# Pads that place the tiles of DMA transfers at multiples of 64 bytes, in an attention and mixture-of-experts kernel

## The chip, the cores and the metric

One core of a Trainium2 chip runs the whole program. The metric is the device time of one execution in microseconds; the time before is the median of three runs.

## The reference

Linear attention is followed by a mixture of experts. For 8 batches and 8 heads of 576 rows with 64 elements:

```
phi(x): p = x @ w_phi;  p = p - max|p|;  [exp(p), exp(-p)]          # 64 -> 256 features
kv = phi(k)^T v;  z = sum of phi(k) over the rows
attn = (phi(q) kv) / (phi(q) z + 1e-6)
x = attn, with the heads side by side                                # 4608 x 512
logits = x @ w_gate                                                  # 8 experts
each (token, expert) in falling order of logits; a token goes to its first expert with room (576)
out[tokens of e] = relu(x[tokens of e] @ w1[e]) @ w2[e]
```

All inputs and the output are fp32.

## The kernel before

**Attention.** The work is cut into 16 units of two batches and two heads. For each unit, `loadx` (L130) fetches k and q into `ki` and `qi` with four DMAs each (`raw`, L116 to 122). One such DMA fills 32 partitions with 36 runs of 32 fp32 values, 128 bytes a run. `loadv` (L123 to 129) fetches v into `vi` in runs of 256 bytes. DVE transposes 32x32 blocks into `kT` and `qT` (L174); PE projects them (L185, tile `g` in PSUM); DVE takes the maximum of the absolute values (L189, tiles `kgm` and `qgm`) and subtracts it (L192, or ACT and POOL at L198 and L201); ACT takes the exponentials into `kP` (L213) and `qP` (L280); PE forms kv (L231), spreads it (L247) and multiplies it with `qP` (L293, the num block, 144 matmuls a unit, `qP` stationary and `kz` moving). DVE divides into a tile `xp` (L309) of 9 rows of 576 bytes a partition, whose bytes 32 to 543 of each row are stored to `xs` in DRAM in runs of 512 bytes (`st`, L312 to 315); the other bytes are parts of the logits.

`ki`, `qi`, `vi`, `kT`, `qT`, `kz` and `xp` have two buffers each, so that the loads of a unit wait for the buffers of the unit two before. The order of all of this is a table of due times, from which the planner `Plan` writes one order for each engine and for SP's queue.

**Routing and experts.** The routing counts logits by digits to find the order of the tokens (`routing`, L582 on). For each of 8 experts, weights are loaded in four chunks for w1 (`raww10` to `raww13`, runs of 1024 bytes) and four for w2 (`raww20` to `raww23`, runs of 2048 bytes) at L767, split into a high and a low part by ACT (L838) and DVE (L841, L842; tiles `w1h`, `w1l`, `w2h`, `w2l`, four each), while POOL gathers the tokens' rows from `xs` into `xg` (L853). From the third expert on, `xg` goes through DRAM (`xd`) and comes back transposed into the tile `xl`. PE computes `h` from `xh`, `xl` (L923) and `y` from `fh`, `fl` (L954), with 576 tokens an expert; the last 64 tokens go through `ff` (L969). ACT copies `y` to `ysb` (L977), and POOL scatters it to the output (L984). The experts follow one another.

**Where tiles lie.** A tile pool reserves a place for each name when it is first asked for, one behind the other, in each partition's memory, and starts every tile at a multiple of 32 bytes. The pools of the first stages (`const`, `mc`, `rt`, `xp` and others) lie first; the attention's pool `att` and the FFN's pool `ffn` use the same memory after them, one after the other in time. The starts, modulo 64, that the program has before and after the change:

| tile | what uses it | before | after |
|---|---|---|---|
| `ki`, `qi` (both buffers) | loads of k and q | 32 | 0 |
| `vi` (both) | loads of v | 0 | 0 |
| `xp`, bytes that a store reads | stores, units 0 to 14 | 0 | 0 |
| `xp` of the last unit, the same | its stores | 32 | 0 |
| `raww10`, `raww11` | loads of w1, chunks 0 and 1 | 0 | 0 |
| `raww12`, `raww13`, `raww20` to `raww23` | the other weight loads | 32 | 0 |
| `xg`, `xl` | gathers, transposed loads | 32 | 0 |
| `ysb` (both) | scatters of the output | 32 | 0 |
| `w`, `bd` | three small loads at the start | 32 | 32 |
| `kT`; `qT` | DVE and PE | 32; 0 | 0; 0 |
| `kz` (two buffers, in turn) | PE, moving | 32, 0 | 0, 32 |
| `xh`, `fh`, `fl`, `ff`, `w1h` to `w2l` | PE, ACT, DVE | 32 | 0 |

`ki` and `qi` start at 224 modulo 256 before and at 0 after; the weight, `xg`, `xl` and `ysb` tiles start at 0 or 32 modulo 256 before, and at 0 after.

Of the kernel before, what the change touches and what calls it, by code (L numbers as in the profile page):

```python
# [7 lines left out]
F32 = mybir.dt.float32  # L8
F32R = mybir.dt.float32r
BF = mybir.dt.bfloat16  # L10
# [87 lines left out]
def attention(ctx, tc, nc, q, k, v, w_phi, w_gate, xs, L, C, xp, cfg={}, after=None, later=None, count=None, init=iter(())):  # L98
# [5 lines left out]
    sb=ctx.enter_context(tc.tile_pool(name='att',bufs=2))  # L104
    ps=ctx.enter_context(tc.tile_pool(name='aps',bufs=1,space=PS))
    ident=C['ident']
    V,A,G,PE=nc.vector,nc.scalar,nc.gpsimd,nc.tensor
# [32 lines left out]
    def pair(u_):  # L140
        return lambda x: ps.tile([128,2,512],F32,name='g%d'%x['buf'][u_],bufs=1)
# [11 lines left out]
    def unit(u):  # L153
        bp,hp=divmod(u,NP)
        t0=u*d['TI']
        def add(name,eng,dur,due,fn,deps=(),mode=None,slot=(),frees=(),lat=None,after=0.,seq=None,ins=0.):
            due=place(name,eng,u,t0+due)
            P.add((name,u),eng,dur,due,fn,[(x,u) for x in deps],
                  lat={'PE':220.,'DVE':95.,'ACT':100.,'POOL':30.,'SP':0.,'X':0.}[eng] if lat is None else lat,mode=mode,slot=slot,frees=frees,after=after,seq=seq and (seq,u),ins=ins)
# [16 lines left out]
        def project(nm,g,s0,s1,due,src):  # L176
            n=s1-s0
            def pe(x):
                p=T[nm+'p',u,g]=pair(('g',u,nm,g))(x)
                t=T[src,u].rearrange('p b s t l -> p b s (t l)')  # L180
                for s in range(s0,s1):
                    for a in range(2):
                        r=slice(64*a,64*a+64)
                        for bi in range(2):
                            PE.matmul(p[64*bi:64*bi+64,a,128*(s-s0):128*(s-s0)+128],t[r,bi,s,:],C['w'][r,:],start=True,stop=True)  # L185
            vw=lambda: T[nm+'p',u,g][:,:,0:128*n].rearrange('p a (s f) -> p a s f',f=128)
            def mx(x):
                m=T[nm+'m',u,g]=sb.tile([128,2,n,1],F32,name=nm+'m',bufs=3)
                V.tensor_reduce(m,vw(),axis=AX.X,op=OP.max,apply_absolute_value=True)  # L189
            def sub(x):  # L190
                t=T[nm+'t',u,g]=sb.tile([128,2,n,128],F32,name=nm+'t',bufs=NT[nm])
                V.tensor_sub(t,vw(),T[nm+'m',u,g].to_broadcast([128,2,n,128]))  # L192
            add((nm,g),'PE',n*(218. if not first else d['cold'][nm]),due,pe,[(src[0]+'t',0),(src[0]+'t',1)],'Q',slots(('g',NG,nm,g)),((src,u),),ins=16*n+.5)
            add((nm+'m',g),'DVE',dv(256*n),due+.8,mx,[(nm,g)])
            if (nm,g) in POOLS and not first:
                def cp(x):
                    t=T[nm+'t',u,g]=sb.tile([128,2,n,128],F32,name=nm+'t',bufs=NT[nm])
                    A.copy(t.rearrange('p a s f -> p a (s f)'),T[nm+'p',u,g][:,:,0:128*n])  # L198
                def gs(x):
                    t=T[nm+'t',u,g]  # L200
                    G.tensor_sub(t,t,T[nm+'m',u,g].to_broadcast([128,2,n,128]))  # L201
                add((nm+'c',g),'ACT',40+ac(256*n),due+1.6,cp,[(nm+'m',g)],slot=slots((nm+'t',NT[nm],g)),frees=(('g',u,nm,g),))
                add((nm+'s',g),'POOL',1450.,due+2.4,gs,[(nm+'c',g)])
            else: add((nm+'s',g),'DVE',dv(256*n),due+1.6,sub,[(nm+'m',g)],slot=slots((nm+'t',NT[nm],g)),frees=(('g',u,nm,g),))
# [79 lines left out]
        for g,(j0,j1) in enumerate(JG):  # L284
            n=j1-j0; due=d['num']+d['ns']*g
            js=sorted(set(j//3 for j in range(j0,j1)))
            def pe(x,g=g,j0=j0,j1=j1):
                p=T['np',u,g]=pair(('g',u,'num',g))(x)
                for a in range(2):
                    for j in range(j0,j1):  # L290
                        for fh in range(2):
                            for ab in range(2):
                                PE.matmul(p[64*ab:64*ab+64,a,73*(j-j0):73*(j-j0)+73],T['qP',u,j//3][:,fh,a,ab,j%3,:],T['kz',u][:,a,fh,ab,:],start=fh==0,stop=fh==1)  # L293
            def dve(x,g=g,j0=j0,j1=j1,n=n):
                p=T['np',u,g][:,:,0:73*n].rearrange('p a (j e) -> p a j e',e=73)
                rd=sb.tile([128,2,n,1],F32,name='rd',bufs=2)
                V.tensor_scalar(rd,p[:,:,:,72:73],1e-6,None,op0=OP.add)
                V.reciprocal(rd,rd)
                if g==0: T['x',u]=(xp if lastu else sb).tile([128,9,144],F32,name='xp',bufs=1 if lastu else 2)
                x_=T['x',u]  # L300
                Lb=L[:,9*bp+j0:9*bp+j1,:]
                if lastu:
                    L3=C['L3'][:,j0:j1]
                    for a in range(2): V.tensor_mul(L3[:,:,:,1+a],p[:,a,:,64*a:64*a+8],rd[:,a].to_broadcast([128,n,8]))
                    V.tensor_reduce(Lb.rearrange('p j (e o) -> p j e o',o=1),L3,axis=AX.X,op=OP.add)
                    if g==1: after()
                    for a in range(2):
                        for j in range(n): A.activation(x_[:,j0+j,8+64*a:72+64*a],p[:,a,j,8-8*a:72-8*a],AF.Copy,scale=rd[:,a,j,:])
                else: V.tensor_mul(x_[:,j0:j1].rearrange('p j (a e) -> p a j e',a=2),p[:,:,:,0:72],rd.to_broadcast([128,2,n,72]))  # L309
            add(('num',g),'PE',n*515.,due,pe,['zk']+[('ex',j) for j in js],'B',slots(('g',NG,'num',g)),tuple(('qP',u,j) for j in js)+(('kz',u),),ins=32*n)  # L310
            add(('x',g),'DVE',(430+dv(144*n)) if not lastu else 900.,due+2.7,dve,[('num',g)],seq=('x',0) if g else None,slot=slots(('xb',2)) if g==0 else (),frees=(('g',u,'num',g),))
# [247 lines left out]
def moe(ctx, tc, nc, L, xs, w1, w2, out, C, MC, R0, rt, cfg={}):  # L559
# [3 lines left out]
    V,G,A,PE=nc.vector,nc.gpsimd,nc.scalar,nc.tensor  # L563
    rp=rt
    fp=ctx.enter_context(tc.tile_pool(name='ffn',bufs=2))
# [16 lines left out]
    def routing(r):  # L582

        last = r==E-1
        wide = r<cfg.get('wide',1)
        if not last:
# [4 lines left out]
            for i,(sh,bits) in enumerate(DIG):  # L591
# [5 lines left out]
                else:  # L597
                    cmp=S([128,NT//n,K,n],f'cmp{K}',BF,b=2)
                    cv=c.rearrange('p (g i) -> p g i',i=n)
                    g=0  # L600
                    for ck in ((WC if K==32 else WC2) if wide else (9,)*(1 if K==32 else 2)):
                        V.tensor_tensor(cmp[:,g:g+ck],cv[:,g:g+ck,None,:].to_broadcast([128,ck,K,n]),
                                        kt[i].rearrange('p (k i) -> p k i',i=n)[:,None].to_broadcast([128,ck,K,n]),op=OP.is_ge); g+=ck
                if wide and i==3: V.memset(fp.tile([1,1],BF,name='wv',bufs=1),0.0)
                if 'rest' in R:
                    with tc.issue_after(R['last']):
                        if i: 
# [90 lines left out]
        lo=S([128,18,64,2],'cmp64',BF,b=2)  # L698
        l2=sf[:,0].rearrange('p (g i) -> p g i',i=2)
        g0=0  # L700
        for lk in (7,7,4) if wide else (9,9):
            g=g0; g0+=lk
            V.tensor_tensor(lo[:,g:g+lk],l2[:,g:g+lk,None,:].to_broadcast([128,lk,64,2]),
                            kl.rearrange('p (k i) -> p k i',i=2)[:,None].to_broadcast([128,lk,64,2]),op=OP.is_equal)
        if wide:

            wk=fp.tile([1,1],BF,name='wk',bufs=1); G.tensor_copy(wk,lo[0:1,0,0,0:1])
        yield
        p=rps([128,9,2,2])
        for g in range(18):  # L710
# [87 lines left out]
    for r in range(1,E):  # L798
# [4 lines left out]
        for i,x in enumerate(z):  # L803
            def f(y,it=it): next(it,None)
            nm=('idx',r) if i==ni else ('up',r) if i>ni else ('rt',r,i)
            if len(x)>2 and x[2]=='ei':

                nm=('ei',r)
# [188 lines left out]
def tile_kernel(ctx, tc, q, k, v, w_phi, moe_w_gate, moe_w1, moe_w2, out):  # L997
# [7 lines left out]
    C['L3'] = L3  # L1005
    C['xd'] = dp.tile([576, 512], F32, name='xd')
    xp = ctx.enter_context(tc.tile_pool(name='xp', bufs=2))
    rp = ctx.enter_context(tc.tile_pool(name='mc', bufs=1))
    rt = ctx.enter_context(tc.tile_pool(name='rt', bufs=1))
    MC, R0 = [], {}  # L1010
# [45 lines left out]
```

## Time and profile before

| | |
|---|---|
| median of 3 runs | 770.24 us (769.56 to 770.79) |
| the profiled execution's own time | 773.05 us |
| its span, first to last instruction | 771.0 us |
| PE, DVE, ACT, POOL busy | 738.6, 572.3, 348.2, 312.0 us |
| mean granted TensorE clock | 0.973 of full speed |
| DMA | 236,944 packets, 94.28 MB; 185,904 packets under 512 bytes |

Attention fills about the first 283 us of the span, the routing the time up to about 310, the experts the rest. PE's busy time is high throughout, and DMA's share is high in the attention stage alone, so a row has to be read with the stretch that it comes from. DMA packets of several queues that wait for one another on an engine are counted each, so that a share can be over 1. A mean time of a packet is worked out from a queue's row as share x length of the stretch x 16 engines / packets; completion marks of a few bytes count as packets too.

### The profile page before, as it was taken

How to read it: one execution, taken by the hardware profiler on the slowest of the kernel's cores; microseconds unless marked ns; L12 is line 12 of the kernel's file. 1: busy time of each engine (PE TensorE's matmuls, PEld its weight loads, DVE VectorE, ACT ScalarE, POOL GpSimd, SP SyncE). 2: the span in 40 equal slices, each digit the busy share in tenths (PEclk: the TensorE clock that was granted, in tenths of full speed). 3: DMA queues.
4: the chain of work that ended last, by engine and by line, in shares of the span. 5: the costliest groups of instructions: out<-in, count | busy, mean ns of one | idle time of the engine just before them, and what ended most of it. 6: DMA issues, size and time to landing. Idle time of an engine off the chain costs nothing.

```text
span 771.0 us, 25322 instructions
## 1 busy us (share of the span) xinstructions
PE 738.6 (96%) x10832; PEld 638.0 (83%) x10832; DVE 572.3 (74%) x1496; ACT 348.2 (45%) x612; POOL 312.0 (40%) x336
## 2 busy tenths in 40 slices
PE   7799999999999976899999999999999999999997
PEld 4578898899988864698898898898898897898995
DVE  5798889998997986788598598597597696673410
ACT  2476766787677640433333333333333423442411
POOL 6587888998889820201302302302202203311002
PEclk9899999999999995899999999999999999999999
DMA  9999889989985131334604504504505505762401
GB/s 135 139 138 147 140 143 173 168 140 149 162 147 116 25 93 56 119 110 140 203 1 147 196 2 150 193 1 155 187 2 167 176 2 170 242 193 71 131 14 48
DMA packets 236944, 94.28 MB, mean 122 GB/s; under 512 B 185904, under 2 KB 223184, under 8 KB 236832
## 3 DMA queue, kind: packets, MB, share of 16 engines
q1 hardware_dynamic: 225552, 71.91, 43.6%
q0 software_dynamic: 6608, 20.16, 8.5%
q8 instruction: 85, 1.39, 0.8%
q10 hardware_dynamic: 4672, 0.59, 0.8%
q14 instruction: 27, 0.22, 0.1%
HBM read 72.58 MB, written 20.05 MB: 120 GB/s over the span
## 4 chain that ended last, share of the span: by engine, by line
PE 70%; issue 12%; DVE 8%; SPq 3%; DMA 2%; POOL 2%; ACT 1%; POOLq 0%; DVEq 0%
PE h L923 21%; PE y L954 18%; PE g L293 9%; PE g L185 5%; PE g L231 4%; PE y L969 3%; DVE kgm L189 3%; SPq L122 3%; PE g L276 2%; PE rps L619 1%; PE g L247 1%; DVE qgm L189 1%; DVE qgt L192 1%; PE rps L615 1%; PE g L260 1%
## 5 line engine op out<-in xcount | busy, mean ns | idle before, releaser
L984 POOL DMA_INDIRECT out_dram<-ysb,idx x40 | 39.3, 981 | 337.2 <-ACT ysb L977 331.2
L222 POOL TENSOR_TENSOR ks<-ks,kP 128x512 f32<-128x512 f32 x112 | 143.2, 1279 | 7.4 <-ACT kP L213 0.2
L923 PE MATMUL h<-xh,w1l 128*128 128x272 f32 (+3 forms) x512 | 142.5, 298 | 0.0
L923 PE MATMUL h<-xh,w1h 128*128 128x272 f32 (+3 forms) x512 | 142.5, 303 | 0.0
L936 ACT ACTIVATE fh<-h 128x272 fp32r<-128x272 f32 (+2 forms) x128 | 48.9, 384 | 137.3 <-PE h L923 129.5
L954 PE MATMUL y<-w2h,fh 128*128 128x512 f32 x256 | 101.1, 398 | 0.0
L954 PE MATMUL y<-w2l,fh 128*128 128x512 f32 x256 | 99.8, 394 | 0.0
L954 PE MATMUL y<-w2h,fl 128*128 128x512 f32 x256 | 99.2, 392 | 0.0
L923 PEld LDWEIGHTS h<-xh,w1h 128*128 128x128 f32 x512 | 96.5, 190 | 2.9 <-ACT fh L936 1.1
L923 PEld LDWEIGHTS h<-xh,w1l 128*128 128x128 f32 x512 | 97.6, 191 | 1.0
L923 PE MATMUL h<-xl,w1h 128*128 128x272 f32 (+3 forms) x512 | 93.4, 299 | 0.0
L213 ACT ACTIVATE kP<-kgt 128x768 f32<-128x768 f32 x96 | 73.9, 837 | 33.4 <-POOL kgt L201 18.9
L940 DVE SCALAR_TENSOR_TENSOR fl<-h,fh 128x272 fp32r<-128x272 f32 (+2 forms) x128 | 53.0, 416 | 39.5 <-ACT fh L936 23.1
L293 PE MATMUL g<-kz,qP 128*64 128x73 f32 x2304 | 79.2, 229 | 2.4 <-DVE kz L262 1.6
L280 ACT ACTIVATE qP<-g 128x768 f32<-128x768 f32 x96 | 71.1, 813 | 21.1 <-PE g L276 21.1
L293 PEld LDWEIGHTS g<-kz,qP 128*64 128x64 f32 x2304 | 76.4, 138 | 4.4 <-DVE kz L262 1.7
L923 PEld LDWEIGHTS h<-xl,w1h 128*128 128x128 f32 x512 | 76.8, 190 | 0.6
L231 PE MATMUL g<-kP,vi 64*64 64x256 f32 x1152 | 71.3, 377 | 0.3 <-PE g L185 0.2
L977 ACT COPY ysb<-y 128x512 f32<-128x512 f32 (+1 forms) x40 | 21.8, 546 | 99.6 <-issue 55.3
L954 PEld LDWEIGHTS y<-w2l,fh 128*128 128x128 f32 x256 | 48.2, 188 | 9.0
L954 PEld LDWEIGHTS y<-w2h,fl 128*128 128x128 f32 x256 | 48.1, 188 | 8.8
L954 PEld LDWEIGHTS y<-w2h,fh 128*128 128x128 f32 x256 | 48.3, 189 | 8.2
(221 smaller groups left out, 1323.7 us busy)
## 6 DMA issues: line engine op xcount, KB each, us to landing
raww<-in_moe_w_dram SPq DMA_DIRECT2D x64, 512.0 KB, 5.2
xs<-xp SPq DMA_DIRECT2D x32, 288.0 KB, 4.7
ki<-in_k_dram SPq DMA_DIRECT2D x62, 144.0 KB, 4.8
qi<-in_q_dram SPq DMA_DIRECT2D x62, 144.0 KB, 4.7
vi<-in_v_dram SPq DMA_DIRECT2D x56, 144.0 KB, 4.7
vi<-in_v_dram POOLq DMA_DIRECT2D x8, 144.0 KB, 7.9
xl<-xd SPq DMA_DIRECT2D x4, 288.0 KB, 4.6
xd<-xg SPq DMA_DIRECT2D x4, 256.0 KB, 2.9
```

The source lines that it names most:

```text
L185: PE.matmul(p[64*bi:64*bi+64,a,128*(s-s0):128*(s-s0)+128],t[r,bi,s,:],C['w'][r,:],start=True,stop=True)
L189: V.tensor_reduce(m,vw(),axis=AX.X,op=OP.max,apply_absolute_value=True)
L213: for i in range(2): A.activation(o[:,:,:,128*i:128*i+128],t,AF.Exp,scale=1.0-2*i)
L222: else: G.tensor_add(ks,ks,kP[:,s])
L231: PE.matmul(p[64*a:64*a+64,i,0:256],v_[r,a,s,:],kP[r,s,a,:],start=s==0,stop=s==8,skip_group_check=True)
L280: for fh in range(2): A.activation(t[:,fh].rearrange('p i a s t -> p i (a s t)'),p,AF.Exp,scale=1.0-2*fh)
L293: PE.matmul(p[64*ab:64*ab+64,a,73*(j-j0):73*(j-j0)+73],T['qP',u,j//3][:,fh,a,ab,j%3,:],T['kz',u][:,a,fh,ab,:],start=fh==0,stop=fh==1)
L923: PE.matmul(p,ws[:,k,o:o+128],xx[:,k,o1:o2],start=n==0,stop=n==11)
L936: A.activation(hh[:,f,o1:o1+m1],p[:,0:m1],AF.Relu)
L940: V.scalar_tensor_tensor(hl[:,f,o1:o1+m1],p[:,0:m1],0.0,hh[:,f,o1:o1+m1],op0=OP.max,op1=OP.subtract)
L954: PE.matmul(p,hx[:,f,o:o+128],ws[:,f%2,:],start=n==0,stop=n==23)
L984: st=G.indirect_dma_start(out=ov,out_offset=bass.IndirectOffsetOnAxis(ap=iv,axis=0),in_=yv,in_offset=None)
```

## The change

Reservations are added or enlarged, and nothing else is touched. In the attention's pool three tiles are asked for that no instruction uses: one behind `kgm`, one behind `qgm` (160 bytes a partition each) and one behind `rd` (32 bytes); in the pool `xp` one of 32 bytes. The tiles `wv` and `wk` in the FFN's pool become 128 elements (256 bytes) in place of one, of which only the first is used, as before.

```diff
             def mx(x):
                 m=T[nm+'m',u,g]=sb.tile([128,2,n,1],F32,name=nm+'m',bufs=3)
+                if u==0 and g==0: sb.tile([128,40],F32,name=nm+'pad',bufs=1)
...
                 rd=sb.tile([128,2,n,1],F32,name='rd',bufs=2)
+                if u==0 and g==0: sb.tile([128,8],F32,name='xpad',bufs=1)
...
-                if wide and i==3: V.memset(fp.tile([1,1],BF,name='wv',bufs=1),0.0)
+                if wide and i==3: V.memset(fp.tile([1,128],BF,name='wv',bufs=1)[:,0:1],0.0)
...
-            wk=fp.tile([1,1],BF,name='wk',bufs=1); G.tensor_copy(wk,lo[0:1,0,0,0:1])
+            wk=fp.tile([1,128],BF,name='wk',bufs=1)[:,0:1]; G.tensor_copy(wk,lo[0:1,0,0,0:1])
...
     xp = ctx.enter_context(tc.tile_pool(name='xp', bufs=2))
+    xp.tile([128, 8], F32, name='xpad', bufs=1)
```

## Rows read from the trace of the kernel before

**Rows 1.** The page, the span in 40 slices: busy tenths of PE and DMA.
```profile
PE   7799999999999976899999999999999999999997
DMA  9999889989985131334604504504505505762401
```
**Rows 2.** Busy time by stretch, first to last us; the first row names the columns.
```profile
core 0: us, PE busy (x) PEld busy (x) DVE busy (x) ACT busy (x) POOL busy (x), PEclk, DMA share, GB/s
0.00:35.00 35.00, 25.55 (x363) 16.72 (x367) 20.79 (x34) 9.48 (x12) 21.22 (x29) 0.90 1.27 136
35.00:90.00 55.00, 52.76 (x1476) 46.39 (x1470) 50.61 (x74) 40.63 (x56) 45.03 (x38) 1.00 0.99 144
...
550.00:607.00 57.00, 57.00 (x455) 49.25 (x455) 43.55 (x148) 19.73 (x42) 10.00 (x16) 1.00 0.35 114
```
**Rows 3.** The chain of waits at the start: start us, length us, what.
```profile
4.55 3.38 SPq L122
...
23.12 1.78 SPq L122
24.95 3.55 DMA ki<-in_k_dram
```
**Rows 4.** Loads of k and q: SP's issue (ns min/median/max); the page's DMA issues (us to landing).
```profile
L122 SPq DMA_DIRECT2D ki<-in_k_dram x62: 311/954/5301, 0.8 to 218.3; - x62
...
ki<-in_k_dram SPq DMA_DIRECT2D x62, 144.0 KB, 4.8
qi<-in_q_dram SPq DMA_DIRECT2D x62, 144.0 KB, 4.7
```
**Rows 5.** The chain of waits in the even part of attention: four num blocks in turn.
```profile
109.00 4.73 PE g L293 x144
...
124.46 4.73 PE g L293 x144
...
139.93 4.74 PE g L293 x144
...
155.40 4.73 PE g L293 x144
```
**Rows 6.** DMA queue, 216 to 217.8 us, k loads alone: packets, MB, share of 16 engines.
```profile
q1 hardware_dynamic: 1813, 0.23, 85.7%
```
**Rows 7.** The same, w1 chunks 0,1 then 2,3 (411.4-414.6, 414.7-419.3; 468.6-471.8, 471.9-476 us).
```profile
q1 hardware_dynamic: 1015, 1.02, 94.6%
...
q1 hardware_dynamic: 1064, 1.05, 71.3%
...
q1 hardware_dynamic: 1003, 1.01, 95.8%
...
q1 hardware_dynamic: 1068, 1.05, 77.9%
```
**Rows 8.** The same, SP's queue in the first 35 us.
```profile
q1 hardware_dynamic: 22497, 2.84, 85.0%
```
**Rows 9.** The same, 432.7 to 436 us, loads of w2.
```profile
q1 hardware_dynamic: 505, 0.99, 85.7%
```
**Rows 10.** Users of kT, then of qT: ns min/median/max, first and last start, forms.
```profile
L185 PE MATMUL g<-w,kT x1152: 269/269/470, 11.4 to 265.6; 64*64 64x128 f32 x192
L174 DVE STREAM_TRANSPOSE kT<-ki x32: 734/768/779, 7.7 to 237.8; 128x576 f32<-128x576 f32 x32
...
L185 PE MATMUL g<-w,qT x1152: 269/269/473, 16.7 to 273.1; 64*64 64x128 f32 x192
L174 DVE STREAM_TRANSPOSE qT<-qi x32: 734/736/781, 15.8 to 250.7; 128x576 f32<-128x576 f32 x32
```
**Rows 11.** Costliest groups: one of three FFN groups each, L923 and L954 (busy us, mean ns).
```profile
L923 PE MATMUL h<-xh,w1h 128*128 128x272 f32 (+3 forms) x512 | 142.5, 303 | 0.0
...
L954 PE MATMUL y<-w2h,fh 128*128 128x512 f32 x256 | 101.1, 398 | 0.0
```

## The prediction

> **What bounds the kernel now.** I read the stages first, then the chain of waits, then the DMA queues in single stretches. The page's slices [rows 1] show PE at 9 tenths or more nearly everywhere after the first 10% of the span, and the DMA engines at 8 or 9 only in the first ten slices or so. So two parts have to be kept apart.
>
> In the first 35 us PE is busy for 25.55 us, and the DMA share is 1.27 (records of several queues overlap) [rows 2]. The chain of waits there is DMA from end to end [rows 3]: from 4.55 us to 24.90 us it is SP's issue of k and q loads, one of which takes up to 5301 ns where the median is 954 [rows 4], because it stands behind earlier loads; then a k load lands at 24.95 + 3.55 = 28.50 us. That is a stretch of about 24 us in which a faster DMA packet would bring the end of the kernel forward. From 35 us on PE is busy for 52.76 us of 55, and from about 100 us the units follow one another in an even beat: the block of 144 num matmuls starts at 109.00, 124.46, 139.93 and 155.40, every 15.47 us [rows 5]. In the MoE stage PE is busy for 57.00 us of 57 [rows 2]. A DMA that lands earlier there gives nothing.
>
> **The change part by part.** Four pads and two enlarged one-element tiles are pure reservations. Line numbers and names of registers aside, the program has the same instructions with the same shapes, order and waits, so nothing is added, removed or moved in any engine's or queue's order, and no wait is added. Only addresses differ. Four classes of access could feel that.
>
> *Loads of k and q.* The starts of `ki` and `qi` go from 32 to 0 modulo 64 (and from 224 to 0 modulo 256). They arrive in runs of 128 bytes, 32 x 36 of them in each of the 124 issues on SP [rows 4], 142,848 in all and the most frequent packet of the kernel. In a short stretch in which k loads run alone, the queue is used at 85.7% of 16 engines for 1.8 us: 24.7 us over 1813 packets, 13.6 ns each, at the misaligned address [rows 6]. What would an aligned one take? No row shows a 128-byte run at a multiple of 64, so I bound it. The nearest rows are the weight loads, since the same queue there writes the same 1024-byte runs, once to `raww10` and `raww11`, which already start at 0 modulo 64, and straight after to `raww12` and `raww13`, which start at 32. In one round the aligned pair takes 94.6% x 3.2 us x 16 / 1015 = 47.7 ns a packet and the misaligned 71.3% x 4.6 x 16 / 1064 = 49.3; in the next it is 48.9 and 47.8 [rows 7]. The sign changes, and the mean difference is under 1%. One per cent of 24 us is 0.2 us. The far end on the side of a gain: in the first 35 us the same 128-byte packets and a few others average 85.0% x 35 x 16 / 22497 = 21.2 ns [rows 8], against 13.6 when alone; if all of that excess came from the placing, 36% of 24 us, 8.6 us, would go. On the side of a loss nothing excludes the same few tenths. I take 0, because the weight loads are the nearest rows, and because 13.6 ns is what the larger packets already lead to: between 13.6 ns for 128 bytes and 48.9 for 1024 the line has 0.0394 ns a byte and 8.6 ns at no bytes, and at 2048 bytes it gives 89; measured is 85.7% x 3.3 us x 16 / 505 = 90 [rows 9]. The misaligned 128-byte and 2048-byte packets and the aligned 1024-byte ones lie on one line, which leaves no room for an extra price of the misaligned ones.
>
> The Trainium skill speaks against this, on its page "DMA: Bandwidth & Descriptors", section "How a descriptor splits into AXI transactions": a run that does not start at a multiple of 256 bytes is fetched from the boundary below it, and a run across such a boundary takes a further transaction; it says so of reads. If writes behaved so, the rows of `ki`, which start at 224 and 96 modulo 256 in turn, would take 11 and 7 beats of 32 bytes, 9 on average, and after the change 4 and 8, 6 on average. The trace disagrees as far as writes go: with 0.0394 ns a byte a beat is 1.26 ns, and 9 beats in place of the 4 of an aligned run would have made the lone k packet 8.6 + 9 x 1.26 = 19.9 ns, where it took 13.6 [rows 6]. By the page the sum would be that of the first rival below, by my rows it is 0.
>
> *Other DMAs.* `raww12`, `raww13`, `raww20` to `raww23`, `xg`, `xl` and `ysb` go from 32 to 0 as well, `vi`, `raww10` and `raww11` stay at 0, and what the stores read of `xp` stays at 0 for 15 of 16 units. All of the moved ones lie in the MoE stage, behind a PE that is busy 57.00 of 57 us. Cost 0; if that cover were gone, under 1% of a load, by the weight packets above.
>
> *TensorE operands.* Moving operands: `kz` alternates between a start at 32 and at 0 from unit to unit, so the row of every second num block is the aligned case. The blocks take 4.73, 4.73, 4.74 and 4.73 us [rows 5], at most 0.01 us in 144 matmuls or 0.07 ns each. Stationary operands: `kT` starts at 32, `qT` at 0, and both have a median of 269 ns a matmul [rows 10]. The FFN's 2304 matmuls in six groups (three of 512, three of 256) [rows 11], whose tiles all go from 32 to 0, then change by less than 2304 x 0.07 = 0.2 us either way. I take 0.
>
> *DVE, ACT, POOL operands.* The transposes to `kT` (32) and `qT` (0) take 734 ns at the least and 779 and 781 at the most [rows 10]; the medians differ (768, 736), but both values occur at both places, and I take them to depend on the instruction ahead. If the medians were due to the place after all, 32 x 32 ns, 1 us of DVE, would go, in part beside PE. I take 0.
>
> Sum: 0 us, between about -0.5 and +0.5 with the near bounds. The profiled execution took 773.05 us with a span of 771.0; the median of the runs is 770.24, 2.81 below it. A difference of 0 against the profiled time is carried over to the median: **770.2 us**.
>
> **The rivals.**
> *The k and q packets do get shorter* (faster). Mechanism: every second 128-byte row of `ki` and `qi` crosses a multiple of 256 bytes before and none after. If a row that crosses costs a second start of a packet, the 8.6 ns of the line above, that is 4.3 ns on the mean, 20% of the 21.2 ns that a packet takes in the crowded start [rows 8] and of the 24 us chain: 4.9 us, 765.3 us. By the Trainium skill's rule in "DMA: Bandwidth & Descriptors", taken for writes, three beats of 1.26 ns would go, 3.8 ns and 4.3 us. For it: the start is bound by nothing else, and packets there are slower than their size explains. Against it: the one line through both kinds of packet, and the overlapping queues as a simpler reason for 21.2 ns. A gain must be over 6% of the packet time to be seen at all (1.5 us of 24).
> *The FFN's matmuls read worse at the new place* (slower). All of their operands move together, each by an odd multiple of 32 bytes, and PE has no slack there. Two more clocks at the 2.4 GHz level that the granted clock of 1.00 stands for are 0.83 ns, times 2304 is 1.9 us: 772.1 us. It decides from 0.67 ns a matmul on (1.54 / 2304). Against it: 0.07 ns between the two places of `kz`. The same mechanism with the other sign gives 768.3.
> *The change does not do what it says.* The constant tiles `w` and `bd`, which a DMA also writes, remain at 32; that is 3 small loads at the start, and gives no change.
>
> **How the numbers follow.** About 0.2%, 1.5 us, is what a measurement of this kernel can tell from no change; its runs spread over 1.2 us. No change: 0.75. Shorter packets in the start, wholly or in part: 0.13; matmuls or DVE steps that become shorter: 0.04; together 0.17 faster. Matmuls or other steps that become longer, or a start whose loads fall out of step: 0.08 slower. The range goes from 767.6, which takes in a part of the first rival, to 771.8, just above the limit of no change.
>
> **What would show it.** Right: lone k packets again at 13.6 ns, the k load of the chain again landing near 28.5 us, num blocks 15.47 us apart, weight packets at 48 to 49 ns in all four chunks. Wrong: k packets of 12 ns or less, or under 19 ns on average in the first 35 us, and a first num block some microseconds earlier; or FFN matmuls whose mean leaves that of [rows 11] by more than a nanosecond.

## The result, and the profile after

The changed kernel takes **761.66 us** (median of 5 runs, 760.43 to 763.97) against 769.56 us (768.84 to 770.79) for the kernel before in the same comparison: a ratio of 0.9898, 95% interval 0.9876 to 0.9919. That is 7.9 us faster, where 770.2 us was forecast with a range from 767.6 to 771.8. The forecast of no change was wrong.

The profiled execution of the changed kernel took 761.66 us with a span of 759.6 us, 11.4 us less than the span before. Where does that come from? First the windows of the profile after, beside [rows 2]:

```profile
core 0: us, PE busy (x) PEld busy (x) DVE busy (x) ACT busy (x) POOL busy (x), PEclk, DMA share, GB/s
0.00:35.00 35.00, 30.05 (x521) 20.65 (x523) 26.89 (x43) 14.37 (x19) 24.19 (x31) 0.90 0.99 168
35.00:90.00 55.00, 51.89 (x1464) 45.19 (x1462) 50.29 (x81) 40.65 (x57) 48.40 (x44) 1.00 0.76 139
...
550.00:607.00 57.00, 57.00 (x456) 49.20 (x456) 43.41 (x149) 19.51 (x43) 10.12 (x15) 1.00 0.35 116
```

In the first 35 us the DMA engines move 168 GB/s in place of 136, at a share of 0.99 in place of 1.27, and PE gets through 521 matmuls in place of 363. From 35 to 90 us about the same bytes a second take a share of 0.76 and not 0.99. From 550 to 607 us nothing has changed. The queue of SP in the first 35 us says the same in packets (after, beside [rows 8]):

```profile
q1 hardware_dynamic: 28963, 3.95, 71.4%
```

71.4% x 35 us x 16 / 28,963 packets is 13.8 ns a packet, where it was 21.2. The chain of waits shows what became of the start (after, beside [rows 3], and the even beat of [rows 5]; the last row is SP's issue of k, beside [rows 4]):

```profile
15.97 4.77 PE g L185 x72
20.74 3.57 PE g L232 x48
...
28.55 2.37 DMA vi<-in_v_dram
...
31.59 1.03 SPq L122
...
32.66 3.09 DMA ki<-in_k_dram
...
100.73 4.73 PE g L294 x144
116.20 4.74 PE g L294 x144
131.67 4.73 PE g L294 x144
```

```profile
L122 SPq DMA_DIRECT2D ki<-in_k_dram x62: 311/852/3087, 0.8 to 209.7; - x62
```

Before, the chain was SP's queue of loads from 4.55 to 24.90 us without a break. Now it is PE's own work from 15.97 to 28.32 us, and loads return to it only after that. The longest wait of an issue of k fell from 5301 to 3087 ns. The beat is the same 15.47 us (100.73, 116.20, 131.67), only 8.3 us earlier than the 109.00 of [rows 5].

The first num block starts at 32.8 us instead of 38.8 and the last num matmul at 273.5 instead of 282.1. (The rows are those of the num line, before and then after: minimum/median/maximum ns of a matmul, first to last start.)

```profile
L293 PE MATMUL g<-kz,qP x2304: 224/226/328, 38.8 to 282.1; 128*64 128x73 f32 x192
```
```profile
L294 PE MATMUL g<-kz,qP x2304: 224/226/278, 32.8 to 273.5; 128*64 128x73 f32 x192
```

So 8.6 of the 11.4 us are gained in attention, 6.0 of them before the first num block. (1.6 us of the 8.6 are one num block that ran long in the trace of before; the last part of the experiments comes back to it.) The other 2.8 us lie behind attention and are not the change's. The windows of before show it:

```profile
320.00:325.00 5.00, 2.98 (x30) 2.46 (x29) 4.03 (x15) 2.64 (x7) 0.00 (x0) 0.92 0.00 0
325.00:330.00 5.00, 5.00 (x32) 4.56 (x32) 4.19 (x14) 0.76 (x2) 0.00 (x0) 0.50 0.00 0
```

PE had work for 2.98 of 5 us in the first expert, then the granted clock stood at 0.50 (the 1.2 GHz level) for 5 us. After shows the same gap some 9 us earlier (311.3 to 316.3 us, 3.31 us busy), with the clock at 1.00 behind it. A later kernel with the changed placing (after_swapped below) has the fall again (0.50 from 315 to 320 us), so it does not go with the place of the tiles. From the start of the last num matmul to the end of the span it takes 488.6 us with the fall, where after takes 486.1 and before 488.9. The medians, 7.9 us apart, fit the gain of attention.

Next to unchanged are the FFN's matmuls (after, beside [rows 11]): 300 and 399 ns where it was 303 and 398. The 3 ns of the first group are more than the nanosecond that the prediction took as a sign against itself, but they are the clock's fall in the first expert and not the place of the tiles: after_swapped, with the changed placing and the fall, has 303 ns again.

```profile
L925 PE MATMUL h<-xh,w1h 128*128 128x272 f32 (+3 forms) x512 | 140.9, 300 | 0.1
...
L956 PE MATMUL y<-w2h,fh 128*128 128x512 f32 x256 | 101.4, 399 | 0.0
```

### The profile page after: what moved, and what is told of

Read it like the earlier page. It is cut to its first block, busy times and chain, and to the rows that moved or that the text cites. A ratio compares the mean times of both kernels' runs of the same rounds, so it can differ in the third digit from the quotient of the medians.

```text
span 759.6 us, 25322 instructions
## 1 busy us (share of the span) xinstructions
PE 732.6 (96%) x10832; PEld 631.2 (83%) x10832; DVE 570.8 (75%) x1496; ACT 347.7 (46%) x612; POOL 312.4 (41%) x336
## 4 chain that ended last, share of the span: by engine, by line
PE 68%; issue 13%; DVE 9%; POOL 5%; ACT 2%; DMA 2%; POOLq 1%; SPq 0%; DVEq 0%; ACTq 0%
PE h L925 21%; PE y L956 18%; PE g L294 8%; PE g L185 4%; PE g L232 3%; DVE kgm L190 3%; PE y L971 3%; PE g L277 2%; PE rps L621 1%; POOL ks L223 1%; PE g L111 1%; DVE qgm L190 1%; DVE qgt L193 1%; PE g L248 1%; ACT kgt L199 1%
## 5 line engine op out<-in xcount | busy, mean ns | idle before, releaser
L986 POOL DMA_INDIRECT out_dram<-ysb,idx x40 | 39.3, 983 | 333.5 <-ACT ysb L979 327.1
L925 PE MATMUL h<-xh,w1h 128*128 128x272 f32 (+3 forms) x512 | 140.9, 300 | 0.1
L942 DVE SCALAR_TENSOR_TENSOR fl<-h,fh 128x272 fp32r<-128x272 f32 (+2 forms) x128 | 53.0, 416 | 38.8 <-ACT fh L938 21.6
L294 PE MATMUL g<-kz,qP 128*64 128x73 f32 x2304 | 77.3, 227 | 1.8 <-DVE kz L263 1.8
L294 PEld LDWEIGHTS g<-kz,qP 128*64 128x64 f32 x2304 | 74.6, 136 | 3.6 <-DVE kz L263 1.9
```

What stands on the lines that cost most here:

```text
L925: PE.matmul(p,ws[:,k,o:o+128],xx[:,k,o1:o2],start=n==0,stop=n==11)
L942: V.scalar_tensor_tensor(hl[:,f,o1:o1+m1],p[:,0:m1],0.0,hh[:,f,o1:o1+m1],op0=OP.max,op1=OP.subtract)
L986: st=G.indirect_dma_start(out=ov,out_offset=bass.IndirectOffsetOnAxis(ap=iv,axis=0),in_=yv,in_offset=None)
```

## The experiments

What the change does to the rows of k and q can be said in three ways. Their start goes from 32 to 0 modulo 64. Every second row crossed a multiple of 256 bytes (rows started at 224 and 96 modulo 256, and 224 + 128 is more than 256), and none does now. And the tiles of the engines moved too. In the expectations, B is always the theory that the crossing is what costs; the others are its rivals, with their numbers beside them. All kernels keep the instructions and their order unless the text says otherwise.

| kernel | starts of k, q / v modulo 256 | us, median (lowest to highest) | ratio to before, 95% |
|---|---|---|---|
| before | 224 / 64 | 770.07 to 771.32 in the five later comparisons | |
| after | 0 / 0 | 761.66 (760.43 to 763.97) | 0.9898 (0.9876 to 0.9919) |
| qk_off32 | 32 / 0 | 768.59 (767.12 to 769.44) | 0.9965 (0.9945 to 0.9985) |
| qk_off64 | 64 / 0 | 767.24 (765.63 to 772.61) | 0.9952 (0.9925 to 0.9980) |
| qk_off16 | 16 / 0 | 782.90 (779.28 to 785.00) | 1.0146 (1.0083 to 1.0208) |
| qk_off128 | 128 / 0 | 762.50 (761.03 to 763.87) | 0.9897 (0.9873 to 0.9921) |
| v_off64 | 0 / 64 | 763.79 (762.02 to 764.40) | 0.9900 (0.9878 to 0.9922) |
| all_off64 | 64 / 64 | 769.30 (767.43 to 771.07) | 0.9984 (0.9970 to 0.9997) |
| ffn_off32 | 0 / 0, FFN's tiles at 32 | 762.92 (761.80 to 765.20) | 0.9898 (0.9842 to 0.9954) |
| before_swapped | 224 / 64 | 769.69 (768.17 to 771.72) | 0.9982 (0.9965 to 1.0000) |
| after_swapped | 0 / 0 | 762.87 (762.23 to 765.81) | 0.9903 (0.9869 to 0.9936) |
| two_pads | 0 / 0 | 764.77 (763.24 to 765.40) | 0.9930 (0.9907 to 0.9953) |
| two_pads_again | 0 / 0 | 762.19 (761.92 to 764.14) | 0.9888 (0.9858 to 0.9918) |
| attention_pads | 0 / 0 | 762.86 (759.98 to 765.54) | 0.9888 (0.9852 to 0.9924) |
| after_again | 0 / 0 | 762.54 (761.54 to 763.65) | 0.9888 (0.9858 to 0.9918) |

**Other starts for k and q.** In the changed kernel `ki` and `qi` are made wider and used from a float of our choice on (8, 16, 4 or 32 floats, which is 32, 64, 16 or 128 bytes):

```diff
-        t=T[nm,u]=sb.tile([128,36,32],F32,name=nm+'i',bufs=2)
+        t=T[nm,u]=sb.tile([128,1216],F32,name=nm+'i',bufs=2)[:,16:16+1152].rearrange('p (g l) -> p g l',l=32)
```

> The changed kernel, but ki and qi alone start 32 bytes past a multiple of 64 (and of 256); every other tile stays where the change put it, kT and qT too. Theory A (a 128-byte run off a multiple of 64 touches three 64-byte words in place of two, and this costs where transfers compete): the whole gain is lost, 769 to 771 us, 128-byte packets of about 21 ns on the mean in the first 35 us, and the k load of the chain lands near 28.5 us again. Theory B (a run that crosses a multiple of 256 costs more): the same, since every second run crosses. Theory C (the place of kT, of the FFN's tiles or of others that the engines read made the gain): 761 to 763 us, as the changed kernel.

> The same with ki and qi 64 bytes past a multiple of 256: runs start at multiples of 64, and every second one still crosses a multiple of 256. Theory A: nothing is lost, 760.5 to 763 us, 128-byte packets at 13 to 14 ns. Theory B: the gain is lost, 769 to 771 us, packets near 21 ns in the first 35 us. Theory C: 761 to 763 us.

> The same with ki and qi 16 bytes past a multiple of 256. Theory A: also three 64-byte words a run, so the same as at 32 bytes, 769 to 771 us. A variant of it in which the price is set by 32-byte pieces (five in place of four at 16 bytes, four at 32 bytes) would make this one slower than the one at 32 bytes, 772 us or more. Theory B: as at 32 bytes, 769 to 771 us. Theory C: 761 to 763 us.

> ki and qi start 128 bytes past a multiple of 256, in the same widened tiles as in the runs at 16, 32 and 64 bytes: no 128-byte run crosses a multiple of 256. Theory B (a run that crosses a multiple of 256 costs more): all of the gain, 760.5 to 763 us, 128-byte packets at 13 to 14 ns in the first 35 us. If the widened tiles themselves, or the exact start at 0, had been what mattered at 64 and 32 bytes: 766 to 769 us again.

With starts at 32 and 64 every second row crosses a multiple of 256 again, and 4 to 6 us of the gain are lost (768.59 and 767.24 us, where ffn_off32 of the same comparison, with `ki` and `qi` at 0, takes 762.92). That is less than the whole gain that theory B gave for k and q alone. With a start at 128 no row crosses, and the whole gain is there. The mean packet of SP's queue in the first 35 us goes along: 19.4 ns at 32, 19.5 at 64 and 14.0 at 128. The starts at 64 and at 128 are both multiples of 64, so it is not the multiple of 64 that counts. The start at 16 goes beyond what a crossing explains: 782.9 us is slower than before, though no more rows cross than at 64. It misses the 769 to 771 us of theory B. Its first num matmul starts at 39.3 us, only 0.5 us later than in before, so what it loses against before comes behind that. The windows of that kernel show the DMA engines busy far into the attention, at a share of 1.16 from 35 to 90 us too:

```profile
35.00:90.00 55.00, 51.92 (x1469) 44.64 (x1461) 50.60 (x73) 39.49 (x54) 43.63 (x36) 1.00 1.16 135
```

**v, and all three.** First `vi` alone is moved to 64 in the same manner (its rows of 256 bytes then all cross). Then a pad of 64 bytes ahead of the attention's pool moves `ki`, `qi` and `vi` together to 64 modulo 256; every tile that a DMA uses there still lies at a multiple of 64, as the change says of itself.

```diff
+    sb.tile([128,16],F32,name='apad',bufs=1)
     w=sb.tile([128,512],BF,name='warm',bufs=1); V.memset(w,0.0)
```

> The changed kernel, but vi alone starts 64 bytes past a multiple of 256, as it did before the change; ki and qi stay at 0. Each 256-byte run of v then crosses a multiple of 256. Theory B: the rest of the gain that ki and qi at 32 bytes did not take away, about 3 us, is lost: 764 to 766 us, 256-byte packets above 18.5 ns on the mean. If v's place is of no account, since it was at a multiple of 64 before and after: 761 to 763 us.

> A pad of 64 bytes ahead of the attention's tiles: ki, qi, vi and all behind them in that pool start at 64 modulo 256, so every DMA tile is still at a multiple of 64. Theory B: nearly all of the gain is lost, 768 to 771 us, as before the change. Theory A (multiples of 64 are what counts): 760.5 to 763 us.

The pad of 64 bytes takes nearly the whole gain away: 769.30 us, 0.9984 of before. This is the sharpest of the runs, since it satisfies the change's own rule. Its windows in the first 35 us are those of before (share 1.25, 135 GB/s; before 1.27 and 136):

```profile
0.00:35.00 35.00, 24.34 (x328) 15.98 (x332) 20.33 (x33) 9.48 (x12) 21.25 (x29) 0.87 1.25 135
```

k and q account for the larger part (qk_off64 gives back 4 to 5 us). v alone gives back 1 to 2 us (763.79 us, where 762.50 is the time of qk_off128 in the same comparison), less than the 3 us that theory B gave for it, and its interval holds the changed kernel too. The two together give back 6.8 of the 8.4 us between before and qk_off128 (770.94, 769.30 and 762.50 us): nearly all of it.

**The FFN's tiles.** `wv` becomes 144 elements, which moves all the FFN's tiles to 32 modulo 64 again:

```diff
-                if wide and i==3: V.memset(fp.tile([1,128],BF,name='wv',bufs=1)[:,0:1],0.0)
+                if wide and i==3: V.memset(fp.tile([1,144],BF,name='wv',bufs=1)[:,0:1],0.0)
```

> The changed kernel, but every tile of the FFN stage (raww, xg, xl, ysb and what the engines read there) starts 32 bytes past a multiple of 64; the attention stage is as after the change. Theories A and B: the loads there lie behind a busy PE, so 761 to 763 us, and the 512-byte runs to xl take about 45 ns in place of 39. Theory C with the FFN's matmuls as the place: the gain is lost in part or whole, 765 to 770 us, spread evenly over the MoE rounds.

762.92 us, the ratio of the changed kernel. The FFN's part of the change is worth nothing that can be measured here; the interval of this run is wide (0.9842 to 0.9954), and attention_pads below says the same with a closer one.

**The order of the loads.** The four loads of a tile go to partitions 0, 32, 64, 96 in turn, and neighbours in the queue may be in each other's way. In these two kernels, made from before and from after, they go to 0, 64, 32, 96:

```diff
-        for a in range(2):
-            for db in range(2):
+        for db in range(2):
+            for a in range(2):
```

> The kernel before, with the four loads of each of k and q issued in the order of partitions 0, 64, 32, 96 in place of 0, 32, 64, 96. Theory P (a crossing costs where loads that follow one another write the same half of the partitions): part of the gain without any change of place, 763 to 768 us. Theory Q (the price belongs to the packet or to its engine, whatever the partitions): 768.5 to 771.5 us, as before.

> The changed kernel with the four loads of each of k and q in the order of partitions 0, 64, 32, 96. Theory B with no price left to avoid: 761 to 763 us, as the changed kernel. If loads that follow one another on the same half of the partitions still hinder one another, as the 1.2 us that the same order gave before the change may say: 759.5 to 761 us.

769.69 and 762.87 us: about 0.2% of a gain in the one (0.35% at the end of its interval), none in the other. This was a miss as a way to more speed, and it excludes the order of the loads as the cause of the gain.

**The price by itself.** A kernel that leaves out everything but loads of k and q: sections of 32 DMAs (36,864 packets of 128 bytes) on SP's and ACT's queue, with a pitch of 128 bytes as in `ki` or of 256, and a start of our choice:

```diff
+    t = big[j][i][:, o:o + 36 * pitch].rearrange('p (g l) -> p g l', l=pitch)[:, :, 0:32]
+    (nc.sync, nc.scalar)[j].dma_start(t[32 * c:32 * c + 32], src)
```

> Leaves out everything but loads of k and q, in 15 sections that wait for one another. A section is 32 loads as the kernel issues them (36 runs of 128 bytes into each of 32 partitions, 36,864 packets), half on SP's queue and half on ACT's, into tiles whose rows have a pitch of 128 or 256 bytes and start at a given place modulo 256. In order: pitch 128 at 0, 64, 32, 16; pitch 256 at 0, 64, 32, 16, 192; pitch 256 at 0 and 192 with each load over all 128 partitions; then on SP's queue alone (16 loads) pitch 256 at 0, 192, 16; then pitch 128 at 0 again. At 13 ns a packet on 16 engines a section takes 30 us. Theory B (a run that crosses a multiple of 256 costs): pitch 128 at 64 and 32 (every second run crosses) 36 to 42 us, pitch 256 at 64 and 32 (none crosses) 30 us like 0, pitch 256 at 192 (every run crosses) 42 us or more. Theory B2 (a start that is no multiple of 128 costs, crossing or not): pitch 256 at 64, 32 and 192 alike, 42 us or more. At 16, where the kernel took 783 us, both leave open whether crossing matters; if it is the start alone, pitch 256 at 16 is above 40 us too. Theory P (the price is paid where 16 engines write into 32 partitions): over 128 partitions 30 us at 192 too; theory Q (price of the packet itself): as dear as in 32 partitions. On one queue alone, theory R (a price only where queues compete): 15 us at 0 and at 192; otherwise 21 us or more at 192.

The windows of this kernel are set to the sections, which carry the same bytes, so that the length of a row is the time of its section. In order: pitch 128 with starts 0, 64, 32, 16; pitch 256 with starts 0, 64, 32, 16, 192; 128 partitions a load with starts 0 and 192; SP's queue alone, half the packets, with starts 0, 192, 16. The last section, the first one again, takes 25.9 us and is left out. The last three columns are clock, DMA share and GB/s.

```profile
1.80:27.60 25.80, 1.28 (x6) 0.00 (x0) 1.00 1.33 183
29.70:61.90 32.20, 1.27 (x6) 0.00 (x0) 1.00 1.58 147
64.20:101.10 36.90, 1.28 (x6) 0.00 (x0) 1.00 1.56 128
103.10:140.90 37.80, 1.28 (x6) 0.00 (x0) 1.00 1.62 125
143.40:168.30 24.90, 1.28 (x6) 0.00 (x0) 1.00 1.27 189
170.60:195.10 24.50, 1.28 (x6) 0.00 (x0) 1.00 1.33 193
197.50:221.50 24.00, 1.27 (x6) 0.00 (x0) 1.00 1.36 197
223.70:265.30 41.60, 1.28 (x6) 0.00 (x0) 1.00 1.65 113
267.90:310.50 42.60, 1.28 (x6) 0.00 (x0) 1.00 1.59 111
313.20:335.60 22.40, 1.47 (x7) 0.00 (x0) 1.00 1.35 211
337.70:380.80 43.10, 1.28 (x6) 0.00 (x0) 1.00 1.57 110
383.10:396.20 13.10, 0.64 (x3) 0.00 (x0) 1.00 1.13 179
398.10:419.30 21.20, 0.64 (x3) 0.00 (x0) 1.00 1.54 111
421.70:441.60 19.90, 0.64 (x3) 0.00 (x0) 1.00 1.61 118
```

At a pitch of 256 no row crosses with starts 0, 64 and 32, and the times are 24.9, 24.5 and 24.0 us: where such a row starts is free. With a start at 192 every row crosses: 42.6 us, 1.7 times as long. At a pitch of 128, as in the kernel, half of the rows cross with starts at 64 and 32: 32.2 and 36.9 against 25.8. Why 32 costs more than 64 there, with as many crossings, stays open. A start at 16 costs 41.6 us without any crossing. At the kernel's pitch, where every second row then crosses, it costs 37.8 us, hardly more than the start at 32 (36.9), so these sections do not explain why the kernel with a start at 16 is 14 us longer than the one at 32. One queue alone shows the same (21.2 against 13.1), and so do loads over 128 partitions (43.1 against 22.4). So neither two queues in each other's way nor the 32 partitions make the price. In time of an engine it is (42.6 - 24.9) x 16 / 36,864 = 7.7 ns for a row that crosses; at the kernel's pitch, worked out the same way over the 18,432 rows that cross, it is 5.6 ns at 64 and 9.6 at 32.

Finer windows of the section with one queue and a start at 192 (its first and second microsecond, then the next ten) show something that bears on the prediction:

```profile
398.10:399.10 1.00, 0.00 (x0) 0.00 (x0) 1.00 1.16 187
399.10:400.10 1.00, 0.00 (x0) 0.00 (x0) 1.00 1.50 121
400.10:410.00 9.90, 0.21 (x1) 0.00 (x0) 1.00 1.60 110
```

Every row of that section crosses, yet its first microsecond goes at 187 GB/s, as fast as rows that do not cross. Only then does the rate fall to 110.

**Longer runs, and stores.** Two more kernels leave out the computation in the same way. In the first the sections of 256 and 512 bytes did not come out as meant: their runs followed one another in DRAM and on the chip, and the trace shows packets of 1024 bytes.

> Leaves out the whole computation: loads alone, in sections of 32 DMAs on two queues, and three sections of stores at the end. Runs of 128 bytes (36,864 a section), 256 (16,384), 512 (8,192), 1024 (4,096) and 2048 (4,096), with starts at 0, 32 or 64 modulo 256. Theory 1 (every further multiple of 256 bytes that a run crosses costs the same, by the earlier run (42.7 - 25.0) us / 36,864 = 0.48 ns of the section): 128 bytes 25 us at 0 and 42 to 43 at 224 and at 160; 256 bytes 7.9 us longer at 64 and at 32 than at 0; 512 bytes 3.9 us longer; 1024 bytes 2.0 us longer; 2048 bytes 2.0 us longer. Theory 2 (it is the packet that costs, and the price is hidden behind the bytes as soon as a run is long): 256 bytes up to 4 us longer, and from 512 bytes on no difference over 1 us. Stores of 512 bytes: by theory 1 also 3.9 us longer, if reading from this memory is split as writing is; no difference, if not.

Its windows by section: 128 bytes with starts 0 and 224 (the section at 160, also 42.6 us, is left out); 1024 bytes with starts 0 and 32; 2048 bytes with starts 0, 32.

```profile
4.60:30.40 25.80, 14.02 (x8) 0.00 (x0) 1.00 1.16 183
32.70:75.30 42.60, 0.00 (x0) 0.00 (x0) 1.00 1.68 111
...
123.40:138.20 14.80, 0.00 (x0) 0.00 (x0) 1.00 0.92 284
157.50:173.40 15.90, 0.00 (x0) 0.00 (x0) 1.00 0.86 263
...
259.70:282.60 22.90, 0.00 (x0) 0.00 (x0) 1.00 0.99 366
284.50:307.40 22.90, 0.00 (x0) 0.00 (x0) 1.00 1.00 366
```

The 128-byte rows repeat the price (42.6 against 25.8). A 1024-byte row that crosses one multiple more takes 7% more at most (15.9 against 14.8; the two other pairs of such sections differ by 4% and by nothing), a 2048-byte row nothing (22.9 and 22.9). Theory 2 of the expectation holds for loads: long rows hide the price. The three sections of stores in this run, in packets of 1024 bytes too, still show one: 380 GB/s with a start at 0 (311 to 319 us), 338 and 339 at 64 and 32 (325 to 333 and 339 to 347 us).

> Leaves out the whole computation: loads alone in seven sections of 32 DMAs on two queues, then stores alone in six, in runs that do not join on the chip's side: 16,384 runs of 256 bytes or 8,192 of 512 a section. Theory 1 (a price for every further multiple of 256 bytes that a run crosses, 0.48 ns of the section by the runs of 128 bytes): loads of 256 bytes 7.9 us longer at 64 and 32 than at 0, of 512 bytes 3.9 us longer. Theory 2 (a price that long runs hide; 1024-byte runs showed 0.2 to 1.1 us more in 15 us for 4,096): 256 bytes 2 to 6 us longer, 512 bytes 0 to 2 us. A start at 16 with 256-byte runs: 4 us or more above the start at 64 in both. Stores: 1024-byte runs showed 1.3 and 1.8 us more in 11.2 us, so 256 bytes 5 to 8 us longer, 512 bytes 2 to 4 us.

In this one the runs are apart on the chip. Its windows: loads of 256 bytes with starts 32 and 16; loads of 512 with starts 0 and 32; stores of 256 with starts 0 and 32, of 512 with starts 0 and 32.

```profile
44.60:64.30 19.70, 0.00 (x0) 0.00 (x0) 1.00 1.28 213
66.70:86.40 19.70, 0.00 (x0) 0.00 (x0) 1.00 1.30 214
88.90:105.10 16.20, 0.07 (x1) 0.00 (x0) 1.00 0.92 262
123.60:140.40 16.80, 0.00 (x0) 0.00 (x0) 1.00 0.89 249
142.50:157.20 14.70, 0.00 (x0) 0.00 (x0) 1.00 1.27 286
177.40:197.00 19.60, 0.04 (x1) 0.00 (x0) 1.00 0.86 213
199.00:211.20 12.20, 0.00 (x0) 0.00 (x0) 1.00 1.15 342
227.10:241.80 14.70, 0.00 (x0) 0.00 (x0) 1.00 0.98 284
```

Loads of 512 bytes take about 4% more when they cross once more (16.8 against 16.2; the section at 0 runs into its neighbour at its end, so this is rough). Stores read the chip's memory, and they pay as well: 19.6 against 14.7 us at 256 bytes and 14.7 against 12.2 at 512. At 256 bytes a start at 16 that crosses costs no more than one at 32. The section of 256-byte loads at 0 was held up by the clearing of the tiles ahead of it, so the price of v's rows by themselves stays open, and the sections at 64 ran into their neighbours and are not read. One thing in them is not explained: the stores of 256 bytes at 64 follow those at 0 without a break, and the rate stays at some 287 GB/s for 4 us behind 157.2 us, where the bytes of the section at 0 end, before it falls to about 215.

**Is that the whole cause?** Of the six edits, two move the rows of k, q and v: the 32 bytes in the pool of `xp` and the 160 behind `kgm`. The kernel before with these two alone:

```diff
+                if u==0 and g==0 and nm=='kg': sb.tile([128,40],F32,name=nm+'pad',bufs=1)
...
+    xp.tile([128, 8], F32, name='xpad', bufs=1)
```

> The kernel before with two of the change's six edits: the 32 bytes in the pool of xp and the 160 bytes behind kgm. They put ki, qi and vi at multiples of 256 bytes; every tile of the FFN but two, xp and kz also lie where the change has them or at another multiple of 32; the pads behind qgm and rd and the enlarged wv and wk are left out. Theory (rows of k, q and v that cross a multiple of 256 bytes are the whole cause): all of the gain, 761 to 763.5 us, and 128-byte packets of the first 35 us at 13.5 to 14 ns. Rival (the other pads have a share, by kz, the FFN's tiles or the stores): 764 to 769 us, with the same 13.5 to 14 ns.

764.77 us, by its letter the rival's number. But its num blocks started with those of the changed kernel, and in the chain of waits it loses time in one place: the num block of unit 3 takes 6.43 us instead of 4.81 (before, two_pads, then after).

```profile
91.83 6.43 PE g L293 x144
```
```profile
85.02 6.43 PE g L294 x144
```
```profile
85.19 4.81 PE g L294 x144
```

So it was run again beside the changed kernel itself and a third one, which has all pads but `wv` and `wk`:

> The changed kernel itself once more, beside the three others of this call. Both theories: 760.5 to 763 us, ratio to before 0.988 to 0.991. In its trace the num block of unit 3 takes 4.8 us, or 6.4 us where the granted clock falls to about half of full speed in it.

> The kernel with two of the six edits once more, beside the changed kernel. Theory (the rows of k, q and v are the whole cause; the 2.5 us that the first run of it lacked are the clock's falls, which vary from execution to execution): within 1.5 us of the changed kernel of the same call, on either side. Rival (the pads behind qgm and rd and the enlarged wv and wk are worth 2 to 3 us, by qP, kz or the FFN's tiles): again 2 to 3 us longer than the changed kernel, with a clear gap between the two intervals.

> The changed kernel with wv and wk of one element as before, that is all pads of the attention and of xp, none in the FFN's pool. Theory (rows of k, q and v alone): within 1.5 us of the changed kernel. Rival: if the two pads behind qgm and rd hold the difference, as the changed kernel; if wv and wk hold it, 2 to 3 us longer than the changed kernel, and as long as the kernel with two edits.

762.19, 762.86 and 762.54 us, three ratios of 0.9888. The rival falls: two pads give the whole gain, and the other four edits nothing that can be measured with intervals of some 2 us to either side. Why the first run of two_pads took 764.77 us is not shown. The long block alone does not explain it, since the trace of two_pads_again has it too (6.43 us at 85.02); three of the four executions of the first run have a mean granted clock of 0.975 (764.26 to 765.40 us) and the fourth 0.98 (763.24 us). The changed kernel itself now shows the long block (the chain, then the window around it, and the window of the short block in after):

```profile
84.82 6.21 PE g L294 x144
```
```profile
84.80:91.10 6.30, 6.28 (x148) 6.20 (x150) 4.22 (x8) 3.23 (x5) 5.91 (x6) 0.76 0.52 90
```
```profile
85.10:90.00 4.90, 4.81 (x146) 4.73 (x148) 4.20 (x8) 3.30 (x5) 4.66 (x4) 1.00 0.36 68
```

The granted clock is 0.76 on average in this block and 1.00 in the short one. So this is a fall of the clock that the same program shows in one execution and not in another, after a stretch in which PE has gaps. The gaps alone don't decide it: in the changed kernel PE is busy for 4.19 us of the 6 ahead of the long block (78.8 to 84.8 us, after_again) and for 4.17 of the 6 ahead of the short one (79.2 to 85.2 us, after). Compared with each other, the two traces that both have the long block, before and after_again, give the gain of attention by itself: the first num matmul at 32.5 us instead of 38.8 and the last at 274.1 instead of 282.1, 8.0 us, and the medians of that comparison differ by 8.0 (770.58 and 762.54).

## Why the prediction was wrong

- **What bounds the kernel** was read rightly for the start: a stretch of DMA in the chain, in which a faster packet brings the end forward. It was cut off too early. Of the 8 us only 6.0 to 6.3 lie ahead of the first num block. In before and after_again 7.0 are gained by the start of unit 3's num block (91.83 and 84.82 us): up to there [rows 2] had a DMA share of 0.99, and I took PE's 52.76 of 55 us as cover. The last microsecond comes late in attention (186.33 and 179.12 us are the starts of a num block there, 7.2 apart; at the end it is 8.0).
- **The step that failed is "Loads of k and q": "I take 0".** The packets of the first 35 us went from 21.2 to 13.8 ns, so nearly all of the excess over 13.6 did come from the placing. The far end of that step, 8.6 us from "all of that excess", was written down and then set aside for two rows that could not show the price. That 8.6 is close to the 8 us gained is in part luck: it was worked out for the first 24 us, and 2 of the 8 us came later.
- The first was the weight packets [rows 7]. They are of 1024 bytes, and there a further crossing costs at most 7% (14.8 to 15.9 us). They were near in queue and address but far in the one thing that matters, the length of the run.
- The second was the k packets "alone" at 13.6 ns [rows 6], which I took for the price at the misaligned place. That stretch is 1.8 us long and has a lull between two loads in it. In the section above, the first microsecond of a burst goes at full rate though every row crosses, and the rate falls after that, while the queue stands. The changed kernel has the same lull at 207.6 to 210.2 us, with rows that do not cross, and its packets take 54.0% x 2.6 us x 16 / 1721 = 13.1 ns: the crossing had cost the lone packet 0.5 ns and the packet of the first 35 us 7.4. So the row showed the packet almost without the price; the 21.2 ns of [rows 8] showed it with the price. The straight line through 128, 1024 and 2048 bytes was a line through three places where it does not show.
- **"Records of several queues overlap"**, the simpler reason for a share of 1.27, is refuted: the same queues have a share of 0.99 after the change, and one queue alone has 1.54 when its rows cross and 1.13 when they do not.
- **The first rival had the right mechanism** and too small a time and chance: 4.9 us at 0.13. Its price for a row, 8.6 ns, is close to the 7.7 ns measured, and its 20% for the mean packet to what SP's queue did: 28,963 packets in the first 35 us in place of 22,497, so 22% less time for each. The term that was mis-sized is the stretch, 24 us of k and q alone, without the units behind it and without v. Nor are `vi`'s starts unmoved in the way that counts. They go from 64 to 0 modulo 256, and my table looked at 64 only.
- On the Trainium skill's page "DMA: Bandwidth & Descriptors", section "How a descriptor splits into AXI transactions", I wrote that the trace disagrees as far as writes go. It agrees in the part that decides here: a run that crosses a multiple of 256 bytes, which by the page takes a further transaction, costs more, in loads and in stores. It does not agree that the bytes below a start are paid for: starts at 64 and 32 take 24.5 and 24.0 us against 24.9 at 0. And the page has nothing that would make a start at 16, inside one 256-byte block, cost 41.6 us.
- **TensorE, DVE, ACT, POOL operands at 0** was right (4.73 us a num block, 15.47 us a beat, 303 ns in the FFN's first group in after_swapped, which has the fall of the clock as before had), and so were the other DMAs of the MoE stage: ffn_off32 moves them back, with no difference. "Slower by FFN matmuls" did not occur.

## What to carry to other kernels

Where short runs (here 128 bytes; for v's 256 bytes the runs show 1 to 2 us at most) are loaded under a standing queue, lay the tile out so that no run crosses a multiple of 256 bytes in the chip's memory. A start at 32, 64 or 128 is free in itself where no run crosses, a start at 16 is not, and "a multiple of 64" is neither needed nor enough. Take the price of a packet from a stretch with a standing queue and with runs of the same length; a brief stretch or a longer packet hides it.

## What was not expected of the hardware

- A start at 16 bytes past a multiple of 32 costs a 128-byte row 1.7 times the time without any crossing (41.6 against 24.9 us). With `ki` and `qi` there the kernel was 1.5% slower than before; as said above, the sections at its own pitch do not explain how much. The Trainium skill, "SBUF — State Buffer", section "Operand start alignment", gives the element size as the rule for a start, and says that this is about legality, not speed; these runs show that speed differs.
- The price of a crossing appears only after about a microsecond of a burst: 187 GB/s in the first, 121 in the second, 110 from then on. Why it comes late was not found out.
- Stores pay for it as well: 20% more at 512 bytes (14.7 against 12.2 us), 33% at 256 bytes (19.6 against 14.7), and at 1024 bytes the rate falls by 11% (380 to 338 GB/s).
- The clock falls in the same place in some executions and not in others: 6.2 to 6.4 us or 4.8 us for the num block of unit 3. This moves a single trace by 1.6 us and should not be read as the effect of an edit.
